# Normalising the product with v by a spread 1/sum in the six float32 attention tiles, and subtracting the low parts of w_r on VectorE

## The chip, the cores and the metric

One core of a Trainium2 chip runs the whole program. The metric is the device time of one execution in microseconds; for the kernel before it is the median of three runs. One of its executions was profiled, and all rows below come from that one.

## The reference

Attention with a local window, global keys and a slope per head, then a channel mix, for 4 batches of 768 rows, 8 heads of 64:

```python
scores = q @ k.T / sqrt(64) + bias                 # per head; masked outside window and globals
a = np.exp(scores - np.max(scores, axis=-1, keepdims=True))
a = a / (np.sum(a, axis=-1, keepdims=True) + 1e-09)
x = (a @ v)                                        # heads side by side: 768 rows of 512
xk = mu_k * x + (1.0 - mu_k) * x_prev              # x_prev: x one row earlier
xr = mu_r * x + (1.0 - mu_r) * x_prev
k = np.maximum(xk @ w_k, 0.0)
out = 1.0 / (1.0 + np.exp(-(xr @ w_r))) * (k * k @ w_v)
```

The weights arrive as 64-bit floats and are brought to float32 on the chip.

## The kernel before

The 3072 rows are 24 tiles of 128 rows; two tiles make a chunk of the channel mix. A step of the main loop (lines 595 to 626) works on three tiles at once: `scores` of tile n, `transposes` of tile n-1 and `weighted` (the product with v) of tile n-2, each in four pairs of heads (hp). Between them `run_ffn` takes pieces of the channel mix of a finished chunk from a generator.

For a pair of heads `scores` multiplies q by k on TensorE into one of two PSUM banks (`ps_s`); VectorE adds the bias pattern and takes the maximum (line 430), ScalarE takes the exp and its sum over the row (line 431), into a tile e. In every second pair, four heads' sums get 1e-9 and are inverted (lines 437 and 438), and each of the four e tiles is multiplied by its 1/sum, on GpSimd (line 444) or, where the set `PLAN["ER"]` says so, on ScalarE (line 442). `transposes` turns e by TensorE (line 456), ScalarE copies the result to SBUF (line 458), and `weighted` multiplies it with v (line 475) into the PSUM bank av, which holds heads on partitions (64 per head) and rows on the free axis. ScalarE copies av into the chunk's tile x (line 486). The first six tiles (n < NATIVE, batch 0) multiply float32 directly, each float32 matmul recorded as two instructions; from tile 6 on q and k are split into high and low parts.

The channel mix of a chunk makes xk and xr from x (`mix`, lines 499 to 504; the high part on ScalarE, the low part xk_lo or xr_lo on VectorE), then kp (96 matmuls of 128x256, lines 511 to 513, in four banks of 24), z and vps. All of these, and the matmuls that make the low parts of three w_k pieces (tiles "rest"), share three PSUM banks (`ps_f`, tag f).

The weights come in ten pieces of 1 MB. Each piece takes three integer steps on VectorE (lines 210 to 212), a copy to the high part on ScalarE (line 216), and the subtraction of the low part (`weight_end`). The string `PLAN["LOW"]` says where: P by TensorE, D on VectorE, G on GpSimd (line 234). Pieces 4 and 5 are w_r.

The order on each engine is made by the tile scheduler from the program and its own cost model, all engines but SP; SP's queue (loads) is in program order in the first six steps. Every engine works its list in order.

Of the kernel before, what the change touches and what calls it, by code (L numbers as in the profile page):

```python
# [9 lines left out]
F32 = mybir.dt.float32  # L10
# [5 lines left out]
ALU = mybir.AluOpType  # L16
# [3 lines left out]
B, H, S, D = 4, 8, 768, 64  # L20
# [4 lines left out]
NATIVE = 6  # L25
# [10 lines left out]

PLAN = {
    "HI": 'AAAAAAAAAA',
    "LOW": 'PPDPGGDDDD',
    "RC": 'AAAAAAAAAAAAAAAAAAAA',  # L40
    "ER": {(0, 1, 0), (0, 3, 0), (1, 1, 0), (1, 3, 0), (2, 1, 0), (2, 3, 0), (3, 1, 0), (3, 3, 0), (4, 1, 0), (4, 3, 0), (5, 1, 0), (5, 3, 0)},
    "ET": (),
    "XC": (),
    "Z": {('q', 0): 'D', ('q', 1): 'A', ('k', 1): 'A'},
    "P0": 'DADDADAD',
# [17 lines left out]
def tile_biased_attention_channel_mix(ctx: ExitStack, tc: tile.TileContext, qT, kT, v, n_sizes, mu_kr, w_k, w_v, w_r, q_rows, k_rows, v_rows, slopes, out):  # L63
    nc = tc.nc
    vec, act, pool, pe = nc.vector, nc.scalar, nc.gpsimd, nc.tensor
# [16 lines left out]
    ident = const.tile([128, 128], F32, name="ident")  # L82
# [18 lines left out]
    s_pool = fast.enter_context(tc.tile_pool(name="sp", bufs=3))  # L101
# [7 lines left out]
    ps_f = fast.enter_context(tc.tile_pool(name="ps_f", bufs=3, space=PSUM))  # L109
# [186 lines left out]
    def pool_copy(dst, src):  # L296
        pool.tensor_scalar(dst, src, 1.0, 1.0, op0=ALU.mult, op1=ALU.mult)  # L297
# [111 lines left out]
    def scores(n, hp):  # L409
        t = n % NT  # L410
        s = state[n]
        c0 = 0 if t else OWN
        w = W - c0
        p = pat if t else pat0
        ps = ps_s.tile([128, 512], F32, name=f"s_{n}_{hp}", tag="s")
        for u in range(2):
            h = 2 * hp + u
            o = ps[:, u * 256 : u * 256 + w]
            if n < NATIVE:
                if t:  # L420
                    pe.matmul(o[:, 0:OWN], s["qr"][:, h, :], state[n - 1]["kr"][:, h, 128 - OWN : 128], start=True, stop=True)  # L421
                pe.matmul(o[:, w - 128 : w], s["qr"][:, h, :], s["kr"][:, h, :], start=True, stop=True)
            else:
                pe.matmul(o, s["qh"][:, h, :], s["kw"][:, h, c0:W], start=True, stop=False)  # L424
                pe.matmul(o, s["ql"][:, h, :], s["kw"][:, h, c0:W], start=False, stop=True)  # L425
        for u in range(2):
            h = 2 * hp + u
            o = ps[:, u * 256 : u * 256 + w]
            e = e_pool.tile([128, W], F32, name=f"e_{n}_{h}", tag="e")
            biased[n, hp] = vec.tensor_tensor_reduce(out=e[:, :w], in0=o, in1=p[:, h, :], op0=ALU.add, op1=ALU.min, scale=-0.125, scalar=3.0e38, accum_out=s["nmax"][:, h : h + 1])  # L430
            act.activation(e[:, :w], e[:, :w], AF.Exp, bias=s["nmax"][:, h : h + 1], scale=-1.0, accum_out=s["sum"][:, h : h + 1])  # L431
            s["e"][h] = e
        if hp % 2 == 0:
            return
        h0, nh = 2 * hp - 2, 4
        r = s_pool.tile([128, nh], F32, name=f"r_{n}_{hp}", tag="r", bufs=8)
        vec.tensor_scalar(r, s["sum"][:, h0 : h0 + nh], 1.0e-9, None, op0=ALU.add)
        vec.reciprocal(r, r)  # L438
        for u in range(nh):
            e = s["e"][h0 + u]  # L440
            if (n, hp, u) in PLAN["ER"]:
                act.mul(e[:, :w], e[:, :w], r[:, u : u + 1])
            else:
                pool.tensor_scalar(e[:, :w], e[:, :w], r[:, u : u + 1], 1.0, op0=ALU.mult, op1=ALU.mult)  # L444
# [16 lines left out]
    def weighted(n, hp):  # L461
        t = n % NT
        s = state[n]
        if hp == 0:
            s["av"] = ps_a.tile([128, 512], F32, name=f"av_{n}", tag="av")
        et = s.pop(("et", hp))
        blocks = s["va"]
        nb = len(blocks)
        for u in range(2):
            h = 2 * hp + u  # L470
            for k, vt in enumerate(blocks):

                q, c, p = k * LATE, (2 * k + u) * 128, vt.shape[0]
                o = s["av"][64 * u : 64 * u + 64, hp * 128 + q : (hp + 1) * 128]
                pe.matmul(o, vt[:, h * 64 : (h + 1) * 64], et[0:p, c + q : c + 128], start=k == 0, stop=k == nb - 1)  # L475
        if hp == 3:
            c, i = divmod(n, 2)
            if i == 0:
                xt = x_pool.tile([128, 4, 257], F32, name=f"x_{c}", tag="x")
                state["x", c] = xt  # L480
                if t == 0:
                    pool.memset(xt[:, :, 0:1], 0.0)
                else:
                    pool_copy(xt[:, :, 0:1], state["x", c - 1][:, :, 256:257])
            xt = state["x", c]
            (vec.tensor_copy if n in PLAN.get("XC", ()) else act.copy)(xt[:, :, 1 + 128 * i : 129 + 128 * i], s["av"].rearrange("p (a q) -> p a q", a=4))  # L486


    def part(pool, tag, n):
# [105 lines left out]
    for step in range(NTILES + 1):  # L595
# [8 lines left out]
        for hp in range(4):  # L604
            if hp == 0 and step > 1:
                for i in range(4):
                    weighted(step - 2, i)
            if hp == 0 and 0 < step < NTILES:
                load_v(step)
            if step:  # L610
                transposes(step - 1, hp)
            if step < NTILES:
                scores(step, hp)
            if hp == 0:
                if step >= LAG and (step - LAG) % 2 == 0:
                    queue.append(ffn((step - LAG) // 2))
                    if len(queue) == 1 and step == LAG:
                        budget[0] = PLAN.get("BUD", -17.5)
            run_ffn(2.5)
            run_ffn(2.5)  # L620
            if hp == 1 and step + 1 < NTILES:
                split_tile(step + 1)
            slot = 4 * step + hp
            weights_load(LOADS[min(slot, len(LOADS) - 1)])
            n = BEGUN[min(slot, len(BEGUN) - 1)]
            weights_go(n, n - 1 if slot < len(BEGUN) else n)
    for i in range(4):
        weighted(NTILES - 1, i)
# [192 lines left out]
```

## Time and profile before

| | |
|---|---|
| median of three runs | 506.63 us (506.36 to 508.09) |
| profiled execution | 506.63 us, of which the span of the profile is 504.9 us |
| busy | TensorE 97%, VectorE 71%, ScalarE 68%, GpSimd 47% |
| DMA | 60.57 MB, mean 120 GB/s |

Times in the rows are microseconds from the start of the span. A timeline row gives the start, the time from the first start to the last end of a run of equal instructions, the engine, line and operation with output and inputs, the count, and in brackets the idle time before it with what ended that. Ends of matmuls are modelled and overlap, so the step between two starts is the better price of one.

### The profile page before, as it was taken

Reading aid. Unit: us, or ns where it says so; the run is one execution under the profiler, and the core shown is the slowest. Engines: PE = TensorE matmul, PEld = TensorE weight load, DVE = VectorE, ACT = ScalarE, POOL = GpSimd, SP = SyncE. Lnnn points to the kernel's source line nnn. Section 1 sums busy time; section 2 is a strip of 40 time slices with the busy share of each in tenths; the row PEclk is TensorE's granted clock in tenths of the full one; section 3 lists DMA queues with packets and bytes.
Section 4 is the critical chain, followed back from the end, with each engine's and each line's share of the span. In section 5 each row is a group of like instructions: output and inputs, shape, how many; then the busy total and the mean of one; then the engine's idle time right before and its main releaser. Section 6 shows DMA issues by size and latency. Waiting matters only on the chain.

```text
span 504.9 us, 10304 instructions
## 1 busy us (share of the span) xinstructions
PE 491.3 (97%) x3590; PEld 432.7 (86%) x3590; DVE 357.5 (71%) x843; ACT 342.1 (68%) x856; POOL 235.6 (47%) x371
## 2 busy tenths in 40 slices
PE   8897999999999999999999999999999999999996
PEld 5575988998998998898898898898898898897985
DVE  7999999668678668658768668748768755447441
ACT  8789678467577577666577677667577678587360
POOL 5357546736546535527547536528447435204000
PEclk9999799999999999999999999999999999999999
DMA  6987522613604503602613613513413215647311
GB/s 215 349 260 275 193 52 66 180 41 86 176 8 104 164 19 88 179 21 79 151 39 81 160 48 81 149 56 81 130 60 80 84 40 164 208 146 272 126 43 48
DMA packets 22586, 60.57 MB, mean 120 GB/s; under 512 B 3296, under 2 KB 4576, under 8 KB 22016
## 3 DMA queue, kind: packets, MB, share of 16 engines
q1 hardware_dynamic: 22384, 59.85, 39.9%
q8 instruction: 30, 0.49, 0.4%
q14 instruction: 28, 0.23, 0.1%
q10 hardware_dynamic: 144, 0.00, 0.0%
HBM read 53.55 MB, written 6.29 MB: 119 GB/s over the span
## 4 chain that ended last, share of the span: by engine, by line
PE 93%; DMA 3%; DVE 2%; ACT 1%; SPq 1%; issue 0%; POOL 0%; ACTq 0%; DVEq 0%
PE kp L511 9%; PE kp L512 9%; PE kp L513 9%; PE vps L511 9%; PE vps L513 9%; PE vps L512 9%; PE av L475 8%; PE t L456 8%; PE z L511 5%; PE z L513 4%; PE z L512 4%; PE s L425 3%; PE s L424 3%; DMA w<-in_w_k_dram 2%; DMA w<-in_w_v_dram 1%; PE s L421 1%
## 5 line engine op out<-in xcount | busy, mean ns | idle before, releaser
L444 POOL TENSOR_SCALAR e<-e,r 128x232 f32<-128x232 f32 (+1 forms) x180 | 97.6, 560 | 148.9 <-DVE r L438 118.5
L512 PE MATMUL kp<-xk_lo,wk 128*128 128x256 f32 x384 | 108.5, 283 | 3.3 <-DVE xk_lo L504 3.3
L511 PE MATMUL kp<-xk_hi,wk 128*128 128x256 f32 x384 | 109.2, 285 | 0.0
L513 PE MATMUL kp<-xk_hi,wk 128*128 128x256 f32 x384 | 108.4, 282 | 0.0
L431 ACT ACTIVATE e<-e,nmax 128x232 f32<-128x232 f32 (+1 forms) x192 | 89.7, 471 | 22.8 <-DVE nmax L430 22.2
L430 DVE CUSTOM_DVE_ANT_0 e<-s,pat 128x232 f32<-128x232 f32 (+1 forms) x192 | 64.7, 373 | 20.4 <-PE s L425 17.4
L511 PE MATMUL vps<-wv,kk_hi 128*128 128x512 f32 (+1 forms) x200 | 77.0, 385 | 0.0
L512 PEld LDWEIGHTS kp<-xk_lo,wk 128*128 128x128 f32 x384 | 73.3, 191 | 3.9 <-DVE xk_lo L504 3.5
L513 PE MATMUL vps<-wv,kk_lo 128*128 128x512 f32 (+1 forms) x200 | 76.6, 383 | 0.0
L512 PE MATMUL vps<-wv,kk_hi 128*128 128x512 f32 (+1 forms) x200 | 76.4, 382 | 0.0
L511 PEld LDWEIGHTS kp<-xk_hi,wk 128*128 128x128 f32 x384 | 73.1, 191 | 0.5
L513 PEld LDWEIGHTS kp<-xk_hi,wk 128*128 128x128 f32 x384 | 73.4, 191 | 0.0
L458 ACT COPY et<-t 128x256 f32<-128x256 f32 (+1 forms) x176 | 56.9, 374 | 11.1 <-PE t L456 10.5
L539 DVE TENSOR_TENSOR kk<-kp,kk 128x512 f32<-128x512 f32 x48 | 33.1, 689 | 40.8 <-ACT kk L538 40.5
L456 PE MATMUL t<-ident,e 128*128 128x128 f32 x352 | 55.4, 277 | 0.2 <-ACT et L458 0.2
L541 DVE TENSOR_TENSOR kk_lo<-kk,kk_hi 128x512 fp32r<-128x512 f32 x48 | 34.0, 709 | 23.1 <-ACT kk_hi L540 22.8
L456 PEld LDWEIGHTS t<-ident,e 128*128 128x128 f32 x352 | 40.6, 136 | 9.4 <-issue 0.7
L486 ACT COPY x<-av 128x512 f32<-128x512 f32 x24 | 14.2, 590 | 45.3 <-PE av L475 45.3
L513 PEld LDWEIGHTS vps<-wv,kk_lo 128*128 128x128 f32 x200 | 37.6, 188 | 7.5
L400 DVE TENSOR_TENSOR ql<-qraw,qh 128x1024 fp32r<-128x1024 f32 x18 | 35.5, 1971 | 11.9 <-POOL qh L297 11.9
L511 PEld LDWEIGHTS vps<-wv,kk_hi 128*128 128x128 f32 x200 | 37.7, 189 | 6.5 <-issue 0.2
L512 PEld LDWEIGHTS vps<-wv,kk_hi 128*128 128x128 f32 x200 | 37.7, 189 | 6.3
(114 smaller groups left out, 1102.2 us busy)
## 6 DMA issues: line engine op xcount, KB each, us to landing
qraw<-in_qT_dram SPq DMA_DIRECT2D x36, 256.0 KB
kraw<-in_kT_dram SPq DMA_DIRECT2D x36, 256.0 KB
out_dram<-sig SPq DMA_DIRECT2D x23, 256.0 KB
va<-in_v_dram SPq DMA_DIRECT2D x20, 240.0 KB
vb<-in_v_dram SPq DMA_DIRECT2D x20, 208.0 KB
w<-in_w_k_dram SPq DMA_DIRECT2D x4, 1024.0 KB
w<-in_w_v_dram SPq DMA_DIRECT2D x4, 1024.0 KB
again<-in_w_k_dram SPq DMA_DIRECT2D x8, 512.0 KB
```

Of the source, the lines that this page charges most:

```text
L400: vec.tensor_sub(ql, s["qr"], qh)
L430: biased[n, hp] = vec.tensor_tensor_reduce(out=e[:, :w], in0=o, in1=p[:, h, :], op0=ALU.add, op1=ALU.min, scale=-0.125, scalar=3.0e38, acc ...
L431: act.activation(e[:, :w], e[:, :w], AF.Exp, bias=s["nmax"][:, h : h + 1], scale=-1.0, accum_out=s["sum"][:, h : h + 1])
L444: pool.tensor_scalar(e[:, :w], e[:, :w], r[:, u : u + 1], 1.0, op0=ALU.mult, op1=ALU.mult)
L456: pe.transpose(pt[0:p, c : c + 128], e[:, k * 128 : k * 128 + p], ident)
L458: (vec.tensor_copy if (n, hp, k) in PLAN.get("ET", ()) else act.copy)(et[0:p, k * 256 : k * 256 + 256], pt[0:p, k * 256 : k * 256 + 256])
L475: pe.matmul(o, vt[:, h * 64 : (h + 1) * 64], et[0:p, c + q : c + 128], start=k == 0, stop=k == nb - 1)
L511: pe.matmul(o, sh, mh, start=first, stop=False)
L512: pe.matmul(o, sh, ml, start=False, stop=False)
L513: pe.matmul(o, sl, mh, start=False, stop=last)
L539: vec.tensor_mul(kk, pv, kk)
L541: rest = vec.tensor_sub(kkl[:, 2 * fp : 2 * fp + 2, :], kk, kkh[:, 2 * fp : 2 * fp + 2, :])
```

## The change

In the six float32 tiles e stays as the exp leaves it. After the last pair of heads the eight sums get 1e-9 and are inverted in one go (r, 128x8). When the product with v is done, ScalarE copies av into x as before; TensorE then makes a bank scale (tag f): for each head the column of r, repeated 64 times, is the stationary operand and the identity the moving one, so that each of 64 partitions holds the head's 1/sum of all 128 rows. VectorE multiplies x by scale in place. `PLAN["ER"]` is empty, so no ScalarE multiplication by 1/sum is left; from tile 6 on the multiplication of e stays on GpSimd as it was. In `PLAN["LOW"]` pieces 4 and 5 (w_r) go from GpSimd to VectorE.

```diff
--- before.py
+++ after.py
@@ -36,9 +36,9 @@
 
 PLAN = {
     "HI": 'AAAAAAAAAA',
-    "LOW": 'PPDPGGDDDD',
+    "LOW": 'PPDPDDDDDD',
     "RC": 'AAAAAAAAAAAAAAAAAAAA',
-    "ER": {(0, 1, 0), (0, 3, 0), (1, 1, 0), (1, 3, 0), (2, 1, 0), (2, 3, 0), (3, 1, 0), (3, 3, 0), (4, 1, 0), (4, 3, 0), (5, 1, 0), (5, 3, 0)},
+    "ER": set(),
     "ET": (),
     "XC": (),
     "Z": {('q', 0): 'D', ('q', 1): 'A', ('k', 1): 'A'},
@@ -430,6 +430,12 @@
             biased[n, hp] = vec.tensor_tensor_reduce(out=e[:, :w], in0=o, in1=p[:, h, :], op0=ALU.add, op1=ALU.min, scale=-0.125, scalar=3.0e38, accum_out=s["nmax"][:, h : h + 1])
             act.activation(e[:, :w], e[:, :w], AF.Exp, bias=s["nmax"][:, h : h + 1], scale=-1.0, accum_out=s["sum"][:, h : h + 1])
             s["e"][h] = e
+        if n < NATIVE:
+            if hp == 3:
+                s["r"] = s_pool.tile([128, H], F32, name=f"r_{n}", tag="r8")
+                vec.tensor_scalar(s["r"], s["sum"], 1.0e-9, None, op0=ALU.add)
+                vec.reciprocal(s["r"], s["r"])
+            return
         if hp % 2 == 0:
             return
         h0, nh = 2 * hp - 2, 4
@@ -483,7 +489,15 @@
                 else:
                     pool_copy(xt[:, :, 0:1], state["x", c - 1][:, :, 256:257])
             xt = state["x", c]
-            (vec.tensor_copy if n in PLAN.get("XC", ()) else act.copy)(xt[:, :, 1 + 128 * i : 129 + 128 * i], s["av"].rearrange("p (a q) -> p a q", a=4))
+            now = xt[:, :, 1 + 128 * i : 129 + 128 * i]
+            act.copy(now, s["av"].rearrange("p (a q) -> p a q", a=4))
+            if n < NATIVE:
+                scale = ps_f.tile([128, 512], F32, name=f"scale_{n}", tag="f")
+                for h in range(H):
+                    g, u = divmod(h, 2)
+                    spread = s["r"][:, h : h + 1].broadcast_to([128, 64])
+                    pe.matmul(scale[64 * u : 64 * u + 64, g * 128 : (g + 1) * 128], spread, ident, start=True, stop=True)
+                vec.tensor_mul(now, scale.rearrange("p (a q) -> p a q", a=4), now)
 
 
     def part(pool, tag, n):
```

The scheduler orders all engines anew. From tile 7's first scores on, the lists agree but for a few neighbours; the differences lie ahead of that. In the rows that follow, lines are those of each kernel's own file, the number behind a letter is the pair of heads (s, t, et) or the head (e), and the last number is a buffer's. Line 504 before is 518 after, 511 to 513 are 525 to 527, 456 is 462, 475 is 481.

VectorE, before, up to the first xk_lo (`_734` is tile 4, w_6 and w_7 are pieces of w_v):

```order
L210 TENSOR_SCALAR wa_648<-w_6_627 128x1024
L437 TENSOR_SCALAR r_1_618<-sum_456 128x4
L430 ISA e_0_739,nmax_626<-s_0_734,pat 128x232
L430 ISA nmax_626 128x1
L430 ISA e_1_742,nmax_626<-s_0_734,pat 128x232
L430 ISA nmax_626 128x1
L210 TENSOR_SCALAR wa_781<-w_7_696 128x1024
L211 SCALAR_TENSOR_TENSOR wa_648<-w_6_627,wa_648 128x1024
L438 RECIPROCAL r_1_618<-r_1_618 128x4
L504 TENSOR_TENSOR xk_lo<-mix_k,xk_hi 128x1024
L211 SCALAR_TENSOR_TENSOR wa_781<-w_7_696,wa_781 128x1024
```

VectorE, after, up to the same xk_lo (`_782`, `_841` are tile 4, pairs 1 and 2; x_694 is the x of chunk 1):

```order
L430 ISA e_2_787,nmax_606<-s_1_782,pat 128x232
L430 ISA nmax_606 128x1
L430 ISA e_3_790,nmax_606<-s_1_782,pat 128x232
L430 ISA nmax_606 128x1
L436 TENSOR_SCALAR r_654<-sum_437 128x8
L211 SCALAR_TENSOR_TENSOR wa_767<-w_7_672,wa_767 128x1024
L430 ISA e_4_846,nmax_606<-s_2_841,pat 128x232
L430 ISA nmax_606 128x1
L430 ISA e_5_849,nmax_606<-s_2_841,pat 128x232
L430 ISA nmax_606 128x1
L518 TENSOR_TENSOR xk_lo<-mix_k,xk_hi 128x1024
L500 TENSOR_TENSOR x_694<-scale_697,x_694 128x4x128
```

Ahead of xk_lo there now stand the bias steps of four more heads of tile 4 and one more integer step (line 211) of piece 7.

VectorE, after, some twenty-five instructions earlier (wr_445 is the first half of w_r, x_381 the x of chunk 0):

```order
L210 TENSOR_SCALAR wa_498<-w_5_496 128x1024
L212 SCALAR_TENSOR_TENSOR wa_441<-w_4_439,wa_441 128x1024
L211 SCALAR_TENSOR_TENSOR wa_498<-w_5_496,wa_498 128x1024
L500 TENSOR_TENSOR x_381<-scale_526,x_381 128x4x128
L430 ISA e_4_622,nmax_438<-s_2_617,pat 128x232
L430 ISA nmax_438 128x1
L430 ISA e_5_625,nmax_438<-s_2_617,pat 128x232
L430 ISA nmax_438 128x1
L212 SCALAR_TENSOR_TENSOR wa_498<-w_5_496,wa_498 128x1024
L234 TENSOR_TENSOR wr_445<-wa_441,wr_445 128x1024
L430 ISA e_6_648,nmax_438<-s_3_643,pat 128x232
L430 ISA nmax_438 128x1
```

Here stand the second of two multiplications by scale ahead of xk_lo and the first of the two subtractions of w_r, the second being between these places (`wr_502`); before, both were on GpSimd.

TensorE, before, at the first matmul that takes xk_lo (s_2_862 is tile 4, pair 2):

```order
L475 MATMUL av_701<-et_3_656,vb_407 64x104
L475 MATMUL av_701<-et_3_656,va_406 64x128
L475 MATMUL av_701<-et_3_656,vb_407 64x104
L421 MATMUL s_2_862<-kz_179,qz_178 128x104
L422 MATMUL s_2_862<-kz_183,qz_178 128x128
L421 MATMUL s_2_862<-kz_179,qz_178 128x104
L422 MATMUL s_2_862<-kz_183,qz_178 128x128
L511 MATMUL kp<-xk_hi,wk_219 128x256 x3
L512 MATMUL kp<-xk_lo,wk_219 128x256
L513 MATMUL kp<-xk_hi,wk_219 128x256
L511 MATMUL kp<-xk_hi,wk_252 128x256
L512 MATMUL kp<-xk_lo,wk_252 128x256
```

This is the end of the list ahead of the channel mix of chunk 0: three matmuls with xk_hi, then the one that takes xk_lo.

TensorE, after, at the same matmul (s_0_987 is tile 5, t_2_1094 is tile 4):

```order
L421 MATMUL s_0_987<-kz_183,qz_182 128x104
L422 MATMUL s_0_987<-kz_188,qz_182 128x128
L421 MATMUL s_0_987<-kz_183,qz_182 128x104
L422 MATMUL s_0_987<-kz_188,qz_182 128x128
L462 MATMUL t_2_1094<-ident,e_4_846 128x128
L462 MATMUL t_2_1094<-ident,e_4_846 104x128
L462 MATMUL t_2_1094<-ident,e_5_849 128x128
L462 MATMUL t_2_1094<-ident,e_5_849 104x128
L526 MATMUL kp<-xk_lo,wk_219 128x256
L527 MATMUL kp<-xk_hi,wk_219 128x256
L525 MATMUL kp<-xk_hi,wk_245 128x256
L526 MATMUL kp<-xk_lo,wk_245 128x256
```

The matmul with xk_lo comes behind tile 5's first scores now.

TensorE, after, the rows some thirty places earlier (t_0_979 is tile 4, av_946 is tile 3, scale_697 is tile 2):

```order
L481 MATMUL av_946<-et_2_834,vb_537 64x104
L525 MATMUL kp<-xk_hi,wk_219 128x256
L499 MATMUL scale_697<-ident,r_493 64x128 x8
L525 MATMUL kp<-xk_hi,wk_219 128x256
L462 MATMUL t_0_979<-ident,e_0_725 128x128
L462 MATMUL t_0_979<-ident,e_0_725 104x128
L462 MATMUL t_0_979<-ident,e_1_728 128x128
L462 MATMUL t_0_979<-ident,e_1_728 104x128
L481 MATMUL av_946<-et_3_899,va_536 64x128
L481 MATMUL av_946<-et_3_899,vb_537 64x104
L481 MATMUL av_946<-et_3_899,va_536 64x128
L481 MATMUL av_946<-et_3_899,vb_537 64x104
```

All transposes and the product with v of tile 3, three pairs of tile 4's transposes, one pair of its product with v, the last pair of its scores, the first pair of tile 5's scores and three batches of scale matmuls stand ahead of the first xk_lo matmul now; before, the scores of tile 4 up to pair 2 were the last ahead of it.

## Rows read from the trace of the kernel before

**Rows 1.** The page, granted TensorE clock in 40 slices of 12.6 us

```profile
PEclk9999799999999999999999999999999999999999
```

**Rows 2.** Busy time by stretch: stretch, length, busy us (instructions) per engine, clock, DMA

```profile
40.00:60.00 20.00, 16.12 (x115) 14.46 (x116) 19.47 (x36) 15.09 (x41) 13.41 (x11) 0.83 0.67 256
```

**Rows 3.** Busy time by stretch, the sum of nine stretches from 60 to 500 us

```profile
sum 440.00, PE 440.00 PEld 394.19 DVE 303.06 ACT 294.46 POOL 201.14; mean PE 48.89 PEld 43.80 DVE 33.67 ACT 32.72 POOL 22.35
```

**Rows 4.** Waits of TensorE: who waited for whom, us in total, times, longest

```profile
PE kp L512 <- DVE xk_lo L504: 3.3, 1, 3.3
PE s L421 <- DVE nmax L430: 2.1, 3, 1.3
...
PE av L475 <- ACT et L458: 0.7, 1, 0.7
PE s L421 <- POOL kz L297: 0.5, 1, 0.5
PE s L422 <- DVE btmp L149: 0.5, 1, 0.5
```

**Rows 5.** Timeline of TensorE, 47 to 60 us

```profile
47.79 0.59 PE L511 MATMUL kp<-xk_hi,wk 128*128 128x256 f32 x3
51.65 0.58 PE L512 MATMUL kp<-xk_lo,wk 128*128 128x256 f32 x1 [3.26 <-DVE xk_lo L504]
...
57.80 0.36 PE L511 MATMUL kp<-xk_hi,wk 128*128 128x256 f32 x1
...
59.53 0.28 PE L513 MATMUL kp<-xk_hi,wk 128*128 128x256 f32 x1
```

**Rows 6.** Timeline of VectorE, 43 to 65 us

```profile
43.62 2.23 DVE L210 TENSOR_SCALAR wa<-w 128x1024 int32<-128x1024 int32 x1
...
46.48 0.68 DVE L210 TENSOR_SCALAR wa<-w 128x1024 int32<-128x1024 int32 x1
...
48.30 3.29 DVE L504 TENSOR_TENSOR xk_lo<-mix_k,xk_hi 128x1024 fp32r<-128x1024 f32 x1
51.52 1.21 DVE L211 SCALAR_TENSOR_TENSOR wa<-w,wa 128x1024 int32<-128x1024 int32 x1
...
63.90 1.21 DVE L504 TENSOR_TENSOR xr_lo<-mix_r,xr_hi 128x1024 fp32r<-128x1024 f32 x1
```

**Rows 7.** Timeline of GpSimd, 42 to 51 us

```profile
42.30 3.00 POOL L234 TENSOR_TENSOR wr<-wa,wr 128x1024 fp32r<-128x1024 f32 x1 [1.90 <-ACT wr L216]
47.15 3.37 POOL L234 TENSOR_TENSOR wr<-wa,wr 128x1024 fp32r<-128x1024 f32 x1 [1.85 <-ACT wr L216]
```

**Rows 8.** Timeline of VectorE, 58 to 62 us

```profile
58.95 1.21 DVE L234 TENSOR_TENSOR wv<-wa,wv 128x1024 fp32r<-128x1024 f32 x1
60.08 0.38 DVE L430 CUSTOM_DVE_ANT_0 e<-s,pat 128x232 f32<-128x232 f32 x1
...
60.39 0.68 DVE L539 TENSOR_TENSOR kk<-kp,kk 128x512 f32<-128x512 f32 x1
61.00 0.38 DVE L430 CUSTOM_DVE_ANT_0 e<-s,pat 128x232 f32<-128x232 f32 x1
```

**Rows 9.** Timeline of TensorE, 80 to 97 us

```profile
80.21 0.60 PE L456 MATMUL t<-ident,e 128*128 128x128 f32 x4
80.65 0.37 PE L421 MATMUL s<-kz,qz 128*128 128x104 f32 x2
...
81.10 0.37 PE L421 MATMUL s<-kz,qz 128*128 128x104 f32 x2
...
94.69 0.45 PE L475 MATMUL av<-et,va 128*64 128x128 f32 x4
94.95 0.36 PE L475 MATMUL av<-et,vb 104*64 104x104 f32 x4
...
96.49 0.65 PE L456 MATMUL t<-ident,e 128*128 128x128 f32 x4
```

**Rows 10.** Groups by line and shape, TensorE's weight loads: x count, busy us, mean ns

```profile
L475 PEld LDWEIGHTS av<-et,va 128*64 128x64 f32 x384 | 25.4, 135 | 8.2 <-issue 4.8 <-ACT et L458 1.2 <-ACT e L431 0.4
```

## The prediction

> **What bounds the kernel now.** I read the clock strip first, then busy time by stretch, then who waits for whom, then the timelines around the one large wait. From 60 to 500 us TensorE is busy in every microsecond: 440.00 of 440 [rows 3]. There no other engine can give a gain, and each matmul more costs its step. The time that is not TensorE's own lies in the front. The granted clock is full except in one slice, the fifth, 50 to 63 us [rows 1]; between 40 and 60 us TensorE is busy 16.12 of 20 us, VectorE 19.47 [rows 2]. So VectorE sets the pace there. TensorE's longest wait of all is 3.3 us, once, for xk_lo on VectorE [rows 4]: it has issued three matmuls with xk_hi at 47.79 and starts the first with xk_lo at 51.65. Behind that wait the clock stands at half (1.2 instead of 2.4 GHz) until about 57.80 [rows 1, 5]. TensorE's other four waits of 0.5 us or more, all ahead of 47.79, sum to 3.8 us [rows 4].
>
> Why xk_lo was late is seen on VectorE. The same subtraction of the same size takes 1.21 us at 63.90, but 3.29 us at 48.30; likewise the integer step of line 210 takes 0.68 us at 46.48 and 2.23 us at 43.62 [rows 6]. Each long one runs beside one of GpSimd's two subtractions of w_r, 42.30 to 45.30 and 47.15 to 50.52, and ends just behind it [rows 7]. Together they cost VectorE 2.08 + 1.55 = 3.63 us.
>
> **The change part by part.**
>
> *VectorE up to the end of xk_lo.* Before, its next instruction starts at 51.52 [rows 6]. The two long ones go back to their free price, since GpSimd has no subtraction of w_r and no scaling of e to do in this stretch any more: -3.63. Added ahead of xk_lo, by the order: two subtractions of w_r at 1.13 (58.95 to 60.08), 2.26; two multiplications by scale, PSUM with SBUF, 128x512, like line 539 at 0.61 (60.39 to 61.00), 1.22; the bias steps of four heads of tile 4 at 0.31 (60.08 to 60.39), 1.24 [rows 8]; one integer step of line 211, 1.21 [rows 6]. That is 5.93, and xk_lo ends at 51.52 - 3.63 + 5.93 = 53.8. The reciprocals, fewer and wider, I put at nothing; they only shorten.
>
> *TensorE up to its first matmul with xk_lo.* By the order it has more to do ahead of it than before at 47.79. Seven groups of four transposes at 0.44 (80.21 to 80.65), 3.08; four heads' scores at 0.45 (80.65 to 81.10), 1.80; the product with v of tile 3, 32 instructions, 1.80 (94.69 to 96.49), and a quarter of tile 4's, 0.45 [rows 9]; three batches of scale. A batch is eight float32 matmuls, so sixteen instructions, with 64 columns standing and 128 moving, the two halves of the array in turn: the shape of the product with v, whose four dearest instructions took 0.26 (94.69 to 94.95) [rows 9]. At 0.065 each a batch is 1.05, three are 3.15. One matmul with xk_hi fewer is -0.12. The sum is 10.2. Of the waits before 47.79, 3.8 us can take some of it [rows 4]: then TensorE is there at 47.79 + 10.2 - 3.8 = 54.2. If nothing is taken up it is 58.0.
>
> The two gates agree, 53.8 and 54.2; I take 54.0. For the product to be ready, the transposes of tiles 3 and 4 no longer wait for GpSimd's scaling, only for the exp; that is why I take the filled end.
>
> *What TensorE is ahead by.* Compare with 57.80 before, where the clock is back. By then it had done 28 kp matmuls and four of tile 3's transposes; after, at 54.0, two kp matmuls, but six more groups of transposes (2.64), the four heads' scores (1.80) and the 2.25 of products with v. The 26 missing kp matmuls are 26 times 0.124 (fourteen from 57.80 to 59.53 in 1.73) [rows 5], 3.2. So after is ahead by 57.8 - 54.0 + 2.64 + 1.80 + 2.25 - 3.2 = 7.3 us, and three batches of scale are still to come, 3.15, in the full stretch, where they cost their whole price. **Net: -4.15 us.** From tile 7's first scores on both kernels have the same list, so the lead stays.
>
> *What costs nothing.* Twelve scalings leave ScalarE and 36 GpSimd; neither engine ends a wait in the full stretch [rows 3]. The four later multiplications by scale, 2.4 us of VectorE, lie beside TensorE's kp, z and vps, as long as VectorE stays ahead of them.
>
> *The batch's price, both ends.* No row shows a repeated column as the standing operand, nor one loaded for the identity. The nearest row from below is the run of the product with v, 0.056 each over 32 (94.69 to 96.49) [rows 9]; from above, a load of 64 columns that nothing hides, 0.135 each [rows 10]. I take 0.065, since shape, type and alternation of halves are those of the run. The ends are -0.9 and +6.7 us for 96 instructions.
>
> A rule of the Trainium skill speaks against this part: TensorEngine Tiling (Array Packing), section Key Properties, has it that changing the tiling mode drains the engine, and a batch of 64 columns stands between others of 128. By the rows the 32 narrow instructions and the step to the wide transpose behind them take 1.80 together [rows 9], so no drain of a matmul's length is in them; by the rule taken at full length the sum would be that of the second rival.
>
> The sum is made against the profiled execution, 506.63 us, which is also the median of the three runs: 506.6 - 4.15 = **502.5 us**.
>
> **The rivals.**
>
> 1. *The front does not close up.* TensorE's extra work ahead of xk_lo finds no gap, because VectorE is at 97% [rows 2] and hands out the scores as late as before. Then it comes to xk_lo at 58.0, four later than forecast, and the time is 506.5. For it: the bias steps of tile 4's first heads stand at much the same place in VectorE's sum. Against: the transposes that move forward wait for exps, which are there.
>
> 2. *The array pays for each change of shape.* Going into a batch and out of it each cost one matmul's own 0.28 us (59.53) [rows 5]; twelve times that is 3.4, and the time 505.9. The skill's rule on draining, above, is this case. Against: the run in rows 9.
>
> 3. *The late gate comes back.* VectorE, with 5.9 us more ahead of xk_lo, or GpSimd's casts for tile 6, which the order now puts right behind the first keys of tile 5, make TensorE wait long enough that the clock falls again. From 51.65 to 57.80 it did 25 kp matmuls and four transposes, worth 25 x 0.124 + 0.44 = 3.5 us, in 6.15 [rows 5]: 2.6 us lost, and the time 505.1.
>
> 4. *Slower: the loads of the repeated column are not hidden.* Each of the 96 new instructions then costs the load's 0.135 instead of 0.065 [rows 10]: 96 x 0.07 = 6.7, and the time 509.2. It decides from 0.124 per instruction on, where the total passes 508.1. For it: a load is longer than the step of any narrow matmul, so something must hide it every time. Against: in the run of the same shape it is hidden every time.
>
> That the change doesn't do what it says can be ruled out by the order: no scaling of e in six tiles, and both subtractions on VectorE.
>
> **How the numbers follow.** A measurement of this kernel can tell 0.3%, 1.5 us, from no change: faster means below 505.1, slower above 508.1. The forecast has 0.60, rival 1 0.15, rival 2 0.05, rival 3 0.08, rival 4 0.12. The forecast is faster almost throughout; rival 3 lies on the border and is split, and so does a part of rival 1, where the front closes up half: faster 0.69, same 0.19, slower 0.12. The range begins at 499.5: VectorE's other steps also run freer of GpSimd and the reciprocals shrink, by 2 us together as an estimate from the 3.6 us that two of them lost, and the batch's lower end gives 0.9. It ends at 507.5, which takes in rivals 1 to 3 and the lower part of rival 4; what is left out is the rest of rival 4 and a front better still.
>
> **What would show it.** Right: xk_lo at 1.2 us on VectorE, ending near 54; TensorE's wait for it under 1 us; no dip in the clock strip near 50 us; a batch of scale near 1.05 us and the multiplication by it near 0.65 us; TensorE busy without a gap from 60 us on. Wrong: a step of over 0.12 us between scale matmuls; a wait of TensorE for a bank that scale holds or for VectorE's multiplication behind 60 us; the first xk_lo matmul at 58 or later; a second stretch at half clock.

## The result, and the profile after

The changed kernel takes 509.73 us, median of six runs (508.48 to 511.63), against 506.66 us for the kernel before in the same session (six runs). The ratio is 1.0058, 95% interval 1.0035 to 1.0081: slower by 3 us, where 502.5 us were forecast. The profiled execution took 508.48 us, its span is 506.6 us. Executions of one kernel differ: those of the kernel before on record run from 503.67 us (mean granted clock 0.998) to 510.33 us (0.986), so a lead that is read from one profile is that execution's.

In the front the clock and the wait for xk_lo came out as forecast, the lead over the kernel before only half. The clock strip of the page, after, has no dip any more; before, it had a 7 in the fifth slice [rows 1]:

```profile
PEclk9999999999999999999999999999999999999999
```

Busy time by stretch, after, columns as in [rows 2]: TensorE is busy 20.00 us of 20 where it was 16.12, GpSimd 1.50 where it was 13.41.

```profile
40.00:60.00 20.00, 20.00 (x202) 18.01 (x201) 20.00 (x53) 18.25 (x53) 1.50 (x3) 1.00 0.65 213
```

TensorE's waits, after. The one for xk_lo, 3.3 us in [rows 4], is gone; 2.0 us of others remain (behind the first row, which is the start of the kernel):

```profile
PE idle L116 <- DVE zeros L113: 1.2, 1, 1.2
PE s L422 <- DVE btmp L149: 1.0, 1, 1.0
PE s L422 <- DVE nmax L430: 0.4, 1, 0.4
PE av L481 <- ACT et L464: 0.4, 1, 0.4
PE s L421 <- DMA qz<-in_qT_dram: 0.2, 1, 0.2
```

VectorE's timeline, after, around the subtraction that was late:

```profile
46.95 0.68 DVE L210 TENSOR_SCALAR wa<-w 128x1024 int32<-128x1024 int32 x1
47.56 1.22 DVE L234 TENSOR_TENSOR wr<-wa,wr 128x1024 fp32r<-128x1024 f32 x1
...
52.31 1.22 DVE L518 TENSOR_TENSOR xk_lo<-mix_k,xk_hi 128x1024 fp32r<-128x1024 f32 x1
53.45 0.68 DVE L500 TENSOR_TENSOR x<-scale,x 128x512 f32<-128x512 f32 x1
```

xk_lo takes 1.22 us instead of 3.29, the integer step 0.68 instead of 2.23 [rows 6]; xk_lo ends at 53.53. TensorE's timeline in the front, after: a batch of scale, and the first matmul with xk_lo, at 55.40, with no wait before it:

```profile
49.64 1.09 PE L499 MATMUL scale<-ident,r 128*64 128x128 f32 x16
50.66 0.39 PE L525 MATMUL kp<-xk_hi,wk 128*128 128x256 f32 x1
...
55.05 0.60 PE L462 MATMUL t<-ident,e 128*128 128x128 f32 x4
55.40 0.36 PE L526 MATMUL kp<-xk_lo,wk 128*128 128x256 f32 x1
```

So the time is lost behind the front, where both kernels have the same list on TensorE, and TensorE is busy in every microsecond of both. What differs there is the price of a step. TensorE's timeline of the kernel before, steady stretch; the first and last rows are the first kp matmul of chunks 2 and 11, the others bound like pieces of the list:

```profile
131.12 0.28 PE L511 MATMUL kp<-xk_hi,wk 128*128 128x256 f32 x1
...
272.33 0.60 PE L456 MATMUL t<-ident,e 128*128 128x128 f32 x4
...
276.65 0.60 PE L456 MATMUL t<-ident,e 128*128 128x128 f32 x4
...
288.17 0.29 PE L511 MATMUL kp<-xk_hi,wk 128*128 128x256 f32 x1
...
291.71 0.60 PE L456 MATMUL t<-ident,e 128*128 128x128 f32 x4
...
471.55 0.28 PE L511 MATMUL kp<-xk_hi,wk 128*128 128x256 f32 x1
```

The same view after:

```profile
129.15 0.28 PE L525 MATMUL kp<-xk_hi,wk 128*128 128x256 f32 x1
...
271.58 0.60 PE L462 MATMUL t<-ident,e 128*128 128x128 f32 x4
...
275.97 0.60 PE L462 MATMUL t<-ident,e 128*128 128x128 f32 x4
...
287.61 0.29 PE L525 MATMUL kp<-xk_hi,wk 128*128 128x256 f32 x1
...
291.18 0.60 PE L462 MATMUL t<-ident,e 128*128 128x128 f32 x4
...
472.96 0.28 PE L525 MATMUL kp<-xk_hi,wk 128*128 128x256 f32 x1
```

At the end of chunk 1 the changed kernel is 131.12 - 129.15 = 1.97 us ahead; nine chunks later, at the first kp matmul of chunk 11, it is 472.96 - 471.55 = 1.41 us behind. The piece between two groups of transposes (four transposes, two heads' scores, 15 vps matmuls) takes 276.65 - 272.33 = 4.32 us before and 4.39 after; a run of 30 kp matmuls 3.54 and 3.57. Groups by line and shape show the same for all matmuls of a kind. Before, 135 to 495 us (x count, busy us, mean ns of one, idle us before):

```profile
L511 PE MATMUL vps<-wv,kk_hi 128*128 128x512 f32 x152 | 59.5, 391 | 0.0
...
L512 PE MATMUL z<-wr,xr_hi 128*128 128x512 f32 x80 | 31.3, 391 | 0.0
```

After, same view and stretch:

```profile
L525 PE MATMUL vps<-wv,kk_hi 128*128 128x512 f32 x152 | 60.3, 397 | 0.0
...
L526 PE MATMUL z<-wr,xr_hi 128*128 128x512 f32 x80 | 31.7, 396 | 0.0
```

Same instruction, same shape, same clock (1.00 from 60 to 500 us in both), 5 to 6 ns dearer. The lists do not explain it: by operation and names of output and inputs, TensorE's are equal from tile 7's first scores to the end. One thing that the change moves stands in no list: **addresses**. The new tag r8 opens three slots of 32 bytes in s_pool, and all buffers of the pools behind it move 96 bytes on in every partition (the addresses are those of the built programs): kk_hi from 187200 to 187296, xk_hi from 195456 to 195552, xr_hi from 204096 to 204192, with their low parts. The weights stay where they are.

### The profile page after: what moved, and what is told of

Its sections match the earlier page's. It is cut to its first block, busy times and chain, and to the rows that moved or that the text cites. A ratio compares the mean times of both kernels' runs of the same rounds, so it can differ in the third digit from the quotient of the medians.

```text
span 506.6 us, 10411 instructions
## 1 busy us (share of the span) xinstructions
PE 498.6 (98%) x3686; PEld 435.5 (86%) x3686; DVE 354.9 (70%) x839; ACT 338.5 (67%) x844; POOL 198.0 (39%) x333
## 4 chain that ended last, share of the span: by engine, by line
PE 96%; DMA 2%; DVE 1%; issue 0%
PE kp L525 9%; PE vps L525 9%; PE kp L526 9%; PE kp L527 9%; PE vps L526 9%; PE vps L527 9%; PE av L481 8%; PE t L462 8%; PE z L525 5%; PE z L527 4%; PE z L526 4%; PE s L425 3%; PE s L424 3%; PE s L422 2%; DMA qz<-in_qT_dram 2%; PE s L421 1%
## 5 line engine op out<-in xcount | busy, mean ns | idle before, releaser
L450 POOL TENSOR_SCALAR e<-e,r 128x232 f32<-128x232 f32 (+1 forms) x144 | 65.0, 469 | 130.2 <-DVE r L444 119.4
L525 PE MATMUL vps<-wv,kk_hi 128*128 128x512 f32 (+1 forms) x200 | 77.6, 389 | 0.0
L526 PE MATMUL vps<-wv,kk_hi 128*128 128x512 f32 (+1 forms) x200 | 77.4, 387 | 0.0
L525 PEld LDWEIGHTS kp<-xk_hi,wk 128*128 128x128 f32 x384 | 72.5, 189 | 1.1 <-issue 0.5
L527 PEld LDWEIGHTS kp<-xk_hi,wk 128*128 128x128 f32 x384 | 72.3, 188 | 0.0
L552 ACT ACTIVATE kk<-kp 128x512 f32<-128x512 f32 x48 | 28.3, 590 | 22.9 <-PE kp L527 22.9
```

The costliest lines, as they stand in the source:

```text
L525: pe.matmul(o, sh, mh, start=first, stop=False)
L526: pe.matmul(o, sh, ml, start=False, stop=False)
L527: pe.matmul(o, sl, mh, start=False, stop=last)
```

## The experiments

Two words first: the standing operand of a matmul is the one that its weight load (PEld in the profile) brings in, the moving one is the other. For vps and z the standing operands are kk and xr and the weights move; for kp a piece of w_k stands and xk moves.

Theory A: the steps of vps, z and kp depend on where kk, xr and xk lie, and the 96 bytes cost the 3 us. The rivals: the loss comes from the work that the change adds or moves (scale, or the low parts of w_r on VectorE).

The table gives all twelve in one; each ratio is to runs of the kernel before on the same chip, whose medians lay between 505.74 and 506.94 us. A step is the mean time from one start to the next of the same product in TensorE's timeline, 135 to 495 us (vps: those of 512 columns; about 420 vps, 211 z, 900 kp). The texts on record give vps as 227, the commonest step before; the mean is 228.6. "Lead" is the start of the last vps matmul of 512 columns in chunk 1, and in chunk 11, against the kernel before in its profiled run (minus: ahead). In after and e2 all buffers behind the new tile in s_pool are moved; in e5, e6, e8 and e12 those of xk, xr and kk and what lies behind them.

| kernel | moved by, bytes | us (ratio, interval) | vps, z, kp step in ns | lead, chunk 1 and 11 |
|---|---|---|---|---|
| before | 0 | 506.66 | 228.6, 232.3, 118.4 | 0, 0 |
| after | 96 | 509.73 (1.0035 to 1.0081) | 234.2, 235.7, 118.8 | -2.0, +1.8 |
| e1 after, old addresses | 0 | 505.48 (0.9957 to 1.0) | 228.6, 232.3, 118.4 | -2.1, -2.1 |
| e2 before, moved | 96 | 510.22 (1.0059 to 1.0124) | 234.2, 235.7, 118.8 | -0.6, +3.2 |
| e3 scale alone | 0 | 510.57 (1.0058 to 1.0104) | 228.8, 232.3, 118.4 | +5.7, +5.7 |
| e4 low parts alone | 0 | 509.62 (1.0048 to 1.0084) | 228.7, 232.3, 118.4 | +2.9, +2.9 |
| e5 e1, moved | 64 | 509.12 (1.0017 to 1.0074) | 233.4, 235.3, 119.7 | -2.2, +2.0 |
| e6 e1, moved | 32 | 510.19 (1.003 to 1.0092) | 233.1, 234.9, 120.5 | -1.3, +3.3 |
| e7 e1, only kk moved | 32 | 507.61 (0.9985 to 1.0048) | 233.1, 232.1, 118.5 | -1.3, +0.7 |
| e8 e1, moved | 128 | 505.10 (0.9929 to 0.9992) | 232.9, 234.7, 115.4 | +0.9, +0.6 |
| e9 e1, only xk moved | 128 | 503.46 (0.9925 to 0.9975) | 228.6, 232.1, 116.4 | -2.0, -3.9 |
| e10 before, only xk moved | 128 | 503.45 (0.9921 to 0.9966) | 228.6, 232.1, 116.3 | -1.4, -3.4 |
| e11 e1, only xk moved | -64 | 507.21 (1.0006 to 1.0031) | 228.6, 232.0, 120.4 | -1.2, +0.5 |
| e12 e1, moved | 512 | 504.91 (0.9958 to 1.0002) | 228.7, 232.3, 118.4 | -2.4, -2.4 |

**e1: the whole change, at the addresses of before.** r takes slots of a tag that exists already; the lists of all engines are those of the change.

```diff
-                s["r"] = s_pool.tile([128, H], F32, name=f"r_{n}", tag="r8")
+                s["r"] = s_pool.tile([128, H], F32, name=f"r_{n}", tag="r", bufs=8)
```

> The changed kernel with its 128x8 reciprocals in the slots of the old tag r, so that all SBUF addresses behind them are those of the kernel before; the lists of all engines are the same as in the changed kernel. Theory A (the 96 bytes by which the xk, xr and kk buffers moved make TensorE's steps longer): the step of vps matmuls falls from 234 to 227 ns and of z from 236 to 232, the lead of 2 us that the changed kernel has at 134 us stays to the end, about 504.5 us, ratio 0.994 to 0.998. Rival B (the steps are longer because the other engines' work lies differently beside them): the steps stay at 234 and 236 ns, about 509.7 us, ratio 1.004 to 1.008.

505.48 us (12 runs), ratio 0.9978, interval 0.9957 to 1.0. TensorE's timeline, the same pieces as above:

```profile
129.07 0.28 PE L525 MATMUL kp<-xk_hi,wk 128*128 128x256 f32 x1
...
270.28 0.60 PE L462 MATMUL t<-ident,e 128*128 128x128 f32 x4
...
274.60 0.60 PE L462 MATMUL t<-ident,e 128*128 128x128 f32 x4
...
286.11 0.29 PE L525 MATMUL kp<-xk_hi,wk 128*128 128x256 f32 x1
...
289.65 0.60 PE L462 MATMUL t<-ident,e 128*128 128x128 f32 x4
...
469.50 0.28 PE L525 MATMUL kp<-xk_hi,wk 128*128 128x256 f32 x1
```

The piece is 4.32 us again, the kp run 3.54, and the lead of 131.12 - 129.07 = 2.05 us at the end of chunk 1 is still there at 471.55 - 469.50 = 2.05. All the loss behind the front is gone with the 96 bytes.

**e2: the kernel before, moved by the same 96 bytes.** A tile that nothing reads, ahead of the other pools; the lists are those of before.

```diff
+    s_pool.tile([128, H], F32, name="pad", tag="pad")
```

> The kernel before with an unused tile of 3 x 32 bytes ahead of the same buffers, so that et, x, xk, xr, kk and sig move by 96 bytes; the lists of all engines are as before. Theory A: vps steps of 234 ns, z of 236, and about 0.4 us more per chunk, 510.5 to 512 us, ratio 1.008 to 1.011. Rival B: 506.7 us, ratio 0.998 to 1.002.

510.22 us, ratio 1.0092 (1.0059 to 1.0124), without a bit of the change's work. TensorE's timeline:

```profile
130.50 0.28 PE L512 MATMUL kp<-xk_hi,wk 128*128 128x256 f32 x1
...
272.92 0.60 PE L457 MATMUL t<-ident,e 128*128 128x128 f32 x4
...
277.31 0.60 PE L457 MATMUL t<-ident,e 128*128 128x128 f32 x4
...
474.30 0.28 PE L512 MATMUL kp<-xk_hi,wk 128*128 128x256 f32 x1
```

The piece takes 4.39 us as in the changed kernel, and this kernel, 0.62 us ahead of the unmoved one at the end of chunk 1, is 474.30 - 471.55 = 2.75 us behind it at the start of chunk 11. With e1 this shows theory A from both sides: the change without the move has the old steps, the move without the change the new ones.

**e3 and e4: the halves of the change, each alone at the old addresses.** e3 has scale, with w_r's low parts on GpSimd as before; e4 is the kernel before with those on VectorE.

```diff
 e3, against e1
-    "LOW": 'PPDPDDDDDD',
+    "LOW": 'PPDPGGDDDD',
 e4, against before
-    "LOW": 'PPDPGGDDDD',
+    "LOW": 'PPDPDDDDDD',
```

> The scaling of the product alone, with the addresses of before: w_r is subtracted on GpSimd again. Theory A and my working of VectorE's list: the two long steps on VectorE come back (3.6 us) and the two subtractions leave it (2.3 us), xk_lo ends 1 to 2 us later than in e1, with a wait of TensorE and perhaps half clock behind it; 505 to 508 us, ratio 0.997 to 1.003. Rival (VectorE's list is not what sets the front): as e1, within 0.5 us.

> The subtraction of w_r on VectorE alone, nothing else; addresses as before. My working: xk_lo ends at 51.5 - 3.6 + 2.3 = 50.2 instead of 51.5 us, TensorE's wait of 3.3 us falls to about 2 or less and the spell at half clock may go (2.6 us): 502 to 505.5 us, ratio 0.991 to 0.998. Rival (the scheduler puts other work in the place, or half clock stays): 505.5 to 507, ratio 0.998 to 1.001.

Both missed: 510.57 and 509.62 us, slower than before and slower than the whole change in e1. The steps are those of before and the lag is constant from chunk 1 on, so both lose in the front. (e3's profiled execution took 512.70 us, the longest of its six, so its lag of 5.7 us is more than the 3.8 us between the medians.) In e3 TensorE's waits have a new longest one, for the bias step of the scores, at 49.3 us:

```profile
PE s L421 <- DVE nmax L430: 2.2, 1, 2.2
```

Its clock strip shows the dip in the fifth slice again (a 7), and two GpSimd subtractions of w_r, at 41.15 and 46.07, still lie beside VectorE's steps: an integer step of line 212 takes 2.96 us at 41.65 there, and 1.21 us at 52.59. xk_lo itself takes 1.21 us. In e4 the first part came as expected: xk_lo ends at 49.77 (50.2 expected), the wait for it falls from 3.3 to 1.6 us, and there is no dip behind it. But there is a new one near 85 us. TensorE's timeline, idle time in brackets:

```profile
83.74 0.44 PE L456 MATMUL t<-ident,e 128*128 128x128 f32 x2 [1.58 <-POOL e L444]
...
85.21 0.50 PE L456 MATMUL t<-ident,e 128*128 128x128 f32 x2 [0.81 <-POOL e L444]
```

The transposes wait for GpSimd's scaling of e, which the new order has put behind the mixing of chunk 1. GpSimd's timeline:

```profile
75.00 2.18 POOL L501 TENSOR_SCALAR mix_k<-x,mus 128x256 f32<-128x256 f32 x4 [7.85 <-ACT x L486]
77.16 3.02 POOL L501 TENSOR_SCALAR mix_r<-x,mus 128x256 f32<-128x256 f32 x4
...
80.48 6.94 POOL L444 TENSOR_SCALAR e<-e,r 128x232 f32<-128x232 f32 x6
```

In e1, with both halves, GpSimd has neither the subtractions nor the scalings of the first six tiles; there the wait for the bias step is 0.2 us and one for the scaling does not occur. So the halves do not add up. How much of it is the missing half and how much only the scheduler's new order of the front, these two runs don't tell apart.

**e5 and e6: 64 and 32 bytes.** The tile ahead of these buffers, which nothing reads, made longer.

```diff
-    f_pool.tile([128, 96], F32, name="ahead", tag="ahead")
+    f_pool.tile([128, 112], F32, name="ahead", tag="ahead")
```

(e6: 104 instead of 112.)

> As e1 (addresses of before), with xk, xr, kk and the buffers behind them moved by 64 bytes; the lists are those of e1. If what counts is the place within 64 bytes, nothing changes: vps step 227 ns, 505.5 us, ratio to before 0.996 to 1.000. If it is the place relative to the weights in a larger period (kk, xr and the weights now start at the same place within 512 bytes), the step goes up by 3 ns or more: over 507 us.

> As e1, the same buffers moved by 32 bytes. Place within 64 bytes: as with 96 bytes, vps step 234, z 236 ns, about 0.35 us more per chunk from tile 7 on, 509.5 us, ratio 1.003 to 1.008. If only the distance counts: something between, 506 to 508 us.

509.12 and 510.19 us. vps is slow at each of the three shifts (233.1, 233.4, 234.2 ns at 32, 64, 96 bytes); kp is slowest at 32 (120.5). The expectation's second case came for e5, its first for e6. None of the three places is as good as the old one, so the old one is a quick spot and not one slot of a 64-byte pattern.

**e7: only kk moved, by 32 bytes.** kk_hi and kk_lo start eight elements into their tiles.

```diff
-GAP = {"kk_hi": 16, "xk_lo": 112}
+GAP = {"kk_hi": 16, "xk_lo": 112, "kk_lo": 8}; FROM = {"kk_hi": 8, "kk_lo": 8}
-        return t[:, 0 : n * 256].rearrange("p (a q) -> p a q", a=n)
+        return t[:, FROM.get(tag, 0) : FROM.get(tag, 0) + n * 256].rearrange("p (a q) -> p a q", a=n)
```

> As e1, only kk_hi and kk_lo (the standing operand of vps) moved by 32 bytes; xk and xr stay. If each matmul's step follows its own standing operand: vps step 234 ns, z stays at 232 and kp at its two common steps of 117 and 118, 508 to 509 us. If it is the buffers that the other engines write beside: z and kp change too, or vps does not.

507.61 us, a little under the 508 to 509 expected. Groups by line and shape, 135 to 495 us: vps is dear, z is not (before, 391 ns each).

```profile
L525 PE MATMUL vps<-wv,kk_hi 128*128 128x512 f32 x152 | 60.2, 396 | 0.0
...
L526 PE MATMUL z<-wr,xr_hi 128*128 128x512 f32 x80 | 31.3, 391 | 0.0
```

So vps follows the place of kk, its standing operand, and z and kp do not. That kp follows xk, its moving operand, is shown by e9 below; for z, whose xr was never moved alone, it follows from its staying the same when kk or xk moves and changing when all three do.

**e8: 128 bytes.** `ahead` has 128 elements.

> As e1, the same buffers moved by 128 bytes. Place within 64 or 128 bytes: as e1, vps step 227 ns, 505.5 us. Larger period: another step.

505.10 us. vps and z are slow as at the other shifts, but kp falls to 115.4 ns, below the kernel before. So the second case came (another step), and the time of the first, 505.5, was met by luck: by the steps, kp's gain and the others' loss differ by 0.2 us in ten chunks. The lead of +0.9 at chunk 1 is that of the profiled execution, 507.56 us, whose clock strip has a dip early in the front:

```profile
PEclk9899999999999999999999999999999999999998
```

At 128 bytes there is thus a place that is better for one product and worse for the others, and it gave the next kernel.

**e9 and e10: only xk moved by 128 bytes,** in the change (with r in tag r) and in the kernel before.

```diff
-GAP = {"kk_hi": 16, "xk_lo": 112}
+GAP = {"kk_hi": 48, "xk_lo": 80}
```

> The change with r in tag r (addresses as before), and only xk_hi and xk_lo 128 bytes further on; kk and xr stay where they are before. Own-address theory (each matmul's step follows the address of its own standing operand): kp's step 115.4 ns as in the shift by 128, vps 227 and z 232 as in the kernel before; 1152 kp matmuls x 3.0 ns = 3.5 us less than the change at the addresses of before (505.5), so 502.0 us (501 to 503.5), ratio 0.988 to 0.995. Rival, spacing (kp was quicker only because all buffers moved together): kp stays at 118.4 and the time at 505.5, ratio 0.996 to 1.0.

> The kernel before with only xk_hi and xk_lo 128 bytes further on, its scaling as before. Own-address theory: kp 115.4 ns, vps 227, z 232; 506.6 - 3.5 = 503.1 us (502 to 504.5), ratio 0.991 to 0.996, and 1 to 2 us more than the change with the same placing. Rival, spacing: 506.6, ratio 0.998 to 1.002.

(The first of these texts calls xk the standing operand; in kp it is the moving one.) 503.46 and 503.45 us: both beat the kernel before, with intervals that end at 0.9975 and 0.9966. TensorE's timeline of e9, the run of 30 kp matmuls: 288.70 - 285.26 = 3.44 us instead of 3.54.

```profile
285.26 0.29 PE L525 MATMUL kp<-xk_hi,wk 128*128 128x256 f32 x1
...
288.70 0.60 PE L462 MATMUL t<-ident,e 128*128 128x128 f32 x4
```

kp's step is 116.4, not 115.4, so the gain was 2.0 us over ten chunks (lead -1.96 to -3.95), not 3.5. That e8 is 1 ns quicker with xk at the same place stays open. The 1 to 2 us between e9 and e10 that the second text expects are not there: with xk in this place the change makes no difference that the times show. In the profiled runs it is 0.5 us ahead of e10 at the end; e10's own front came out 1.4 us quicker than that of the kernel before, though nothing of its edit was meant for the front. Its wait for the bias steps is 0.7 us, 2.1 in [rows 4], and its granted clock between 40 and 60 us is 0.91, where [rows 2] have 0.83; over 20 us that is 1.6 us at full clock. Why it differs is not shown.

```profile
40.00:60.00 20.00, 15.99 (x126) 14.34 (x127) 19.54 (x37) 16.47 (x43) 14.38 (x9) 0.91 0.65 244
```

**e11 and e12: is it the remainder by 512?** In the kernel before, kk and xr lie, like their weights wv and wr, at addresses that leave 320 when divided by 512 bytes; xk leaves 384, wk 320. e11 moves xk alone to 320; e12 moves all three by 512.

```diff
 e11, against e1
-GAP = {"kk_hi": 16, "xk_lo": 112}
+GAP = {"kk_hi": 0, "xk_lo": 128}
 e12, against e1
-    f_pool.tile([128, 96], F32, name="ahead", tag="ahead")
+    f_pool.tile([128, 224], F32, name="ahead", tag="ahead")
```

> The change with r in tag r, and only xk_hi and xk_lo 64 bytes nearer, so that xk, like kk and xr, has the same remainder as its weights when its address in the partition is divided by 512 (320). If equal remainders are the quick place in general, kp's step falls below 118.4 ns as in the shift by 128 (115 to 116.5), vps and z stay at 228.6 and 232.3, and the time is 503 to 504.5 us (ratio 0.992 to 0.997). If that is chance and each product has a place of its own, kp's step is 118 to 121 and the time 505 to 508 (ratio 0.997 to 1.004).

> The change with r in tag r, and xk, xr, kk and the tiles behind them 512 bytes further on. If the step depends on the address with a period that divides 512, all three steps are those of the change at the addresses of before (vps 228.6, z 232.3, kp 118.4 ns) and the time 505.5 us (ratio 0.995 to 1.0), with no drift between chunk 1 and chunk 11. If distance or another period counts, vps is at 233 or more and the time 508 to 511 (ratio 1.002 to 1.009).

e12 came out as the period expects, 504.91 us with all steps as in e1. Its timeline has the piece at 4.32 us and the kp run at 3.54:

```profile
269.94 0.60 PE L462 MATMUL t<-ident,e 128*128 128x128 f32 x4
...
274.26 0.60 PE L462 MATMUL t<-ident,e 128*128 128x128 f32 x4
...
285.77 0.29 PE L525 MATMUL kp<-xk_hi,wk 128*128 128x256 f32 x1
...
289.31 0.60 PE L462 MATMUL t<-ident,e 128*128 128x128 f32 x4
```

In e11 the second case came: 507.21 us, kp at 120.4 ns. Its run of 30 kp matmuls takes 291.21 - 287.61 = 3.60 us:

```profile
287.61 0.29 PE L525 MATMUL kp<-xk_hi,wk 128*128 128x256 f32 x1
...
291.21 0.60 PE L462 MATMUL t<-ident,e 128*128 128x128 f32 x4
```

Equal remainders are the quickest of the places tried for vps and z, and one of the slow ones for kp, whose moved operand is the moving one.

## Why the prediction was wrong

**VectorE's gate: right.** xk_lo was to end at 53.8 and ended at 53.53; both instructions that ran beside GpSimd went back to their free price (1.22 and 0.68 us).

**TensorE's gate: late by 1.4 us.** Forecast 54.2, taken as 54.0; measured 55.40, with no wait before it, so TensorE's own list sets it. The step "Of the waits before 47.79, 3.8 us can take some of it" was read as all. In TensorE's timeline all idle times ahead of 47.79, the start at 1.2 us left out, sum to 4.5 us before, and those ahead of 55.40 to 2.1 after: 2.4 were filled. The sum of work is then 55.40 - 47.79 + 2.4 = 10.0, where 10.2 were forecast, so the work was right and the filling too high; that goes part of the way to rival 1's 58.0.

**The clock: right.** No dip, and no wait for xk_lo; all six executions of the changed kernel have a mean granted clock of 0.997 or more.

**The batch of scale: right.** From its first instruction to the next kp it takes 50.66 - 49.64 = 1.02 us against 1.05 forecast, 64 ns for each of 16 with both changes of shape within (the 1.09 us of the row are to its last, modelled end). The rivals that made it dear (2 and 4) fall. The Trainium skill, TensorEngine Tiling (Array Packing), section Key Properties, says that a change of tiling mode drains the engine; these rows show no drain of a matmul's length.

**The lead: half.** 4.15 us forecast, 2.05 measured at the end of chunk 1 in e1, where the addresses are those of before. The late gate is 1.4 of the difference. The other 0.7 us lie between the gate and the end of chunk 1: there the forecast had 0.34 us less work than before (2.64 + 1.80 + 2.25 - 3.2 - 3.15), and e1 took 0.3 us more. By the steps in TensorE's timeline the three batches cost 3.16 us as forecast, but 24 transposes fewer saved 2.2 us instead of 2.64, 40 instructions fewer of the product with v 1.9 instead of 2.25, and 26 kp matmuls more cost 3.4 instead of 3.2. At this point the forecast would have been 506.6 - 2.05 = 504.6 us, within the range; e1 measured 505.48.

**The step that failed** is "From tile 7's first scores on both kernels have the same list, so the lead stays". The list is the same, the prices are not. By the steps of the table a chunk of 48 vps, 24 z and 96 kp costs 48 x 5.6 + 24 x 3.4 + 96 x 0.4 = 389 ns more, nine chunks 3.5 us; chunk 11 has only 24 vps of 512 columns and adds 0.25. That is 3.8 us, and the lead went from -2.0 to +1.8, also 3.8. The same sum gives the drift of the other kernels: for e7 2.1 us (measured 2.0), for e6 4.7 (4.6), for e5 4.2 (4.15), for e9 -2.0 (-2.0). No rival had it. It could have been seen: the diff adds a tag to a pool, and lines 57 and 123 of the kernel before hold sizes that nothing reads (GAP and ahead), which set the places of just these buffers.

So the side effect on addresses costs 3.8 us by the steps. What the change itself is worth is not shown as clearly: 2 us in e1's profiled front, 1.3 us between the medians of e1 and before with an interval that ends at 1.0, and nothing between e9 and e10.

## What to carry to other kernels

Where TensorE is busy throughout and a change allocates anything in SBUF, compare the addresses of the matmuls' operands before and after, and cost nothing as "the same list" until they agree; to test an arithmetic change, keep the old addresses (put the new tile into a tag that exists, as e1 does). When a loss grows evenly with every chunk, look at the step between two starts of equal instructions instead of at waits. And since the place is a parameter of its own, try it on purpose: 128 bytes on for one operand gave 2 us by the steps here, as much as the change or more (3.5 by the medians of e10 and before, of which 1.4 in the profiles lie in the front and not in the steps).

## What the runs showed of the hardware

A float32 matmul's step depended on the SBUF address of its operands, with the same instruction lists and the granted clock full: for vps (512 columns) 228.6 ns at the old place and 232.9 to 234.2 at 32, 64, 96 and 128 bytes further on; for z 232.3 against 234.7 to 235.7 at the same four; for kp (256 columns), by the shift of xk, 120.4 (-64), 118.4 (0), 120.5 (32), 119.7 (64), 118.8 (96), 115.4 to 116.4 (128), and 118.4 again at 512. So all that was seen fits a pattern that repeats every 512 bytes; a shift of 256 was not tried. Whether the address itself counts or its place against the other operand's, and what in the chip makes it, was not tried: the weights were never moved. The weight loads of vps, z and kp took 188 to 189 ns before and after.

The Trainium skill, SBUF — State Buffer, section Operand start alignment, asks only that an operand starts at a multiple of its element size, and says of its rule: "This is about legality, not speed". All addresses here keep that rule; the runs add that there is a price besides it: between the quickest and the slowest place seen, 2% of the step of vps and 4% of that of kp.

Unexpected too was that the halves of a change can each be slower than none (e3, e4), where the whole at the same addresses is not (e1).
